# Attention followed by a gated product on one core: the products take the batches in pairs, one half of d_ff at a time

## The chip, the cores and the metric

The kernel runs on one core of a Trainium2 chip. The time is the device time of the whole kernel in microseconds (us). TensorE is called PE below (and PEld where it loads weights), VectorE DVE, ScalarE ACT, GpSimd POOL, and SyncE, which issues all DMAs here, SP.

## The reference

Causal attention over 4 batches, 12 heads, 448 positions, head dimension 64, all float32:

```
scores = where(mask, -1e9, (q @ k.T) / 8)
attn   = exp(scores - max) ; attn = attn / (sum + 1e-9)
x      = (attn @ v), the heads side by side: 1792 tokens x 768
out    = ((x @ w_a) * (x @ w_b)) @ w_out        # 768 -> 1536 -> 768
```

The weights arrive as 64-bit words, which the kernel turns into float32 on the chip with integer and float operations.

## The kernel before

**Units.** The weights come in 36 units of 128 x 768: 12 of w_a and 12 of w_b, alternating (units 0 to 23), and 12 of w_out (24 to 35). `load_words` fetches the 64-bit words of a unit, `convert_unit` makes float32 of it (five DVE operations and one of ACT, lines 303 to 315) and keeps a copy in DRAM (`w_keep`). `load_kept` fetches that copy again when the unit is used a second time. `split_unit` splits a unit into a high part (`w_hi`, ACT, line 255) and a rest (`w_lo`, DVE, line 271); attention's output x and the gated product g are split in the same way. A product of one 128-row slice k is then three matmuls of 448 columns, high x high, high x rest, rest x high (`products`, line 498), and a unit for one batch is 18 of these.

**Attention of two heads.** A step works on a pair of heads of a batch; there are 24 pairs of heads. `scores` multiplies q and k in four blocks of rows (line 375), takes the negative maximum on DVE (388) and the exponential with its sum on ACT (394), forms the reciprocal of the sum on DVE (408, 411) and normalises on POOL (419). `turn` transposes the causal part of each head in 10 PE operations (440): 7 work on 128 rows of the array, 3 on 64 rows, the lower half of a block on the diagonal. ACT copies the result out of PSUM in two pieces per head (255, `pt<-t`). `values` multiplies with v (461), and ACT and DVE split the result into `x_hi` and `x_lo`. Three buffers `p` hold the heads between the maximum and the transposition.

**Order.** `order` (line 476) lists which unit is used for which batch: units 0 to 13 for batch 0 alone, 14 to 23 for batches 0 and 1 in turn, 0 to 13 for batch 1, units 24 to 35 for batches 0 and 1, then all 36 for batch 2 and all 36 for batch 3. Attention of batch 0 stands in front of the products; that of batches 1, 2 and 3 is dealt out among them by `attend`, one pair of heads every 11, 26 and 34 slices k (`AT`). Three units are converted in front (`PACE`). Every operation is entered with an estimated duration, and `Plan.order` (line 123) puts the operations of each engine in an order by a list schedule: among the operations that are ready by its estimates it takes the one entered first. Each engine, and SP's DMA queue, then works through its list in order. PSUM has three banks `m` for products (batch 0's scores use them too), two for scores, two for transposes and one for values.

Of the kernel before, what the change touches and what calls it, by code (L numbers as in the profile page):

```python
# [18 lines left out]
P = 128  # L19
# [6 lines left out]
UW = KT * P  # L26

# [6 lines left out]
SOLO = 14  # L34

APART = (3, 0, 0, 0)


AT = ((2, 11), (262, 26), (436, 34))
STEP = (8, 3, 8)  # L40

LATE = (27, 2)

PACE = (0, 1, 1, 1, 0, 0, 0)
LEAD = (3, 2)
# [3 lines left out]
HOLD = (10e3, 5e3)  # L49
# [166 lines left out]
def causal_attention_then_gated_product(  # L216
# [24 lines left out]
    ident = const.tile([P, P], F32, name="ident")  # L241
    mask = const.tile([P, S], F32, name="mask")
# [3 lines left out]
    g_hi = const.tile([P, FT, S], F32R, name="g_hi")  # L246
    g_lo = const.tile([P, FT, S], F32R, name="g_lo")
    w_keep = [dram.tile([P, UW], F32, name=f"w_keep{u}") for u in range(NU)]

    g_keep = [dram.tile([P, S], F32, name=f"g_keep{f}") for f in range(FT)]  # L250
# [26 lines left out]
    w_64, w_32, w_parts = {}, {}, {}  # L277

    def load_words(u):
        t = sb("w_64", 3, [P, UW, 2], U32)  # L280
        load(P * UW * 8, lambda: t.t.rearrange("p n t -> p (n t)"), lambda: w[u].bitcast(U32), [], [t])
        w_64[u] = t

    def load_kept(n):
        t = sb("w_32", 3, [P, UW])
        u = fetched[n]
        load(P * UW * 4, lambda: t.t, lambda: w_keep[u], [("keep", u)], [t])
        w_32[n] = t

    def convert_unit(u, n=None):  # L290
        t = w_64.pop(u)
# [11 lines left out]
        plan.op("dve", dve_ns(UW, 2), lambda: nc.vector.tensor_scalar(  # L303
            out=e.t, in0=high(), scalar1=0x7FF00000, scalar2=None, op0=ALU.bitwise_and), [t], [e])
        plan.op("dve", dve_ns(UW, 2), lambda: nc.vector.tensor_scalar(
            out=m.t, in0=high(), scalar1=0x000FFFFF, scalar2=0x00100000,
            op0=ALU.bitwise_and, op1=ALU.bitwise_or), [t], [m])
        plan.op("act", act_ns(UW), lambda: nc.scalar.activation(
            e.t, e.t, AF.Copy, bias=-896.0 * 2**23, scale=8.0), [e], [e])
        plan.op("dve", dve_ns(UW), lambda: nc.vector.scalar_tensor_tensor(  # L310
            out=r(), in0=m.t, scalar=2.0**32, in1=low(), op0=ALU.mult, op1=ALU.add), [m, t], [m])
        plan.op("dve", dve_ns(UW), lambda: nc.vector.scalar_tensor_tensor(  # L312
            out=e.t, in0=high(), scalar=0x80000000, in1=e.t,
            op0=ALU.bitwise_and, op1=ALU.bitwise_or), [t, e], [e])
        plan.op("dve", dve_ns(UW), lambda: nc.vector.scalar_tensor_tensor(  # L315
# [3 lines left out]
        if n is not None:  # L319
            w_32[n] = wt  # L320

    def split_unit(n):
        if n >= len(fetched):
            return
        t = w_32.pop(n)
# [8 lines left out]
        w_parts[n] = hi, lo  # L334
# [17 lines left out]
    def scores(b, hp):  # L352
# [14 lines left out]
        for pair, w0 in (((3, 0), 448), ((2, 1), 320)):  # L367
            banks = [bank("m", 3) if b == 0 and w0 == 320 else bank(f"s{j}") for j in range(2)]
# [44 lines left out]
        for ci in pairs.values():  # L413
            for j in range(2):
                for i in ci:
                    def norm(i=i, j=j, p=p_of[b, hp, j]):
                        s = rc.t[:D if i == 0 else P, j, i:i + 1]
                        pc = chunk(p, i)
                        return nc.gpsimd.tensor_scalar(  # L419
# [3 lines left out]
                    plan.op("pool", pool_ns(QE[i]), norm, [(rc, j, i)], [(p_of[b, hp, j], i)])  # L423


    spots = (((0, 0), (3, 448)), ((1, 0), (2, 320)))

    def turn(b, hp, j):
        p = p_of.pop((b, hp, j))
        for n, spot in enumerate(spots):  # L430
            t = bank(f"t{n}")
            for c, o in spot:
                for i in range(c, 4):

                    q0 = max(QS[i], 128 * c)
                    r = slice(q0 - QS[i], P)
                    at = o + q0 - 128 * c

                    def mm(c=c, i=i, r=r, at=at, t=t):
# [6 lines left out]
                    plan.op("pe", (P - r.start) / 1.2, mm, [(p, i), "ident"], [t])  # L446
            full = sb("pt", 6, [P, 512])
            copy("act", 512, lambda full=full: full.t, lambda t=t: t.t, [t], [full], True)
            pt[j, n] = full

    def values(b, hp, x):
        ps, vt = bank("pv"), v_of.pop((b, hp))
        x_hi, x_lo = x
        parts = dict(pt)
        for c in range(4):
# [3 lines left out]
            def mm(c=c, n=n, o=o):  # L459
                for j in range(2):  # L460
# [8 lines left out]
        copy("act", S, lambda: x_hi.t[:, hp, :], lambda: ps.t[:, :S], [ps], [(x_hi, hp)], True)  # L469
        two_input("dve", S, lambda: x_lo.t[:, hp, :], lambda: ps.t[:, :S],  # L470
                  lambda: x_hi.t[:, hp, :].bitcast(F32), ALU.subtract, [ps, (x_hi, hp)], [(x_lo, hp)])
# [4 lines left out]
    order = (  # L476
        [(0, u) for u in range(SOLO)]
        + [(b, u) for u in range(SOLO, NA) for b in range(2)]
        + [(1, u) for u in range(SOLO)]
        + [(b, u) for b in range(2) for u in range(NA, NU)]  # L480
        + [(b, u) for b in range(2, B) for u in range(NU)]
    )

    fetched = [u for n, (b, u) in enumerate(order) if n == 0 or order[n - 1][1] != u]
    xs, a_sb, g_wait = {}, {}, []
# [4 lines left out]
    def part_g(f, g, key):  # L490
        copy("act", S, lambda: g_hi[:, f, :], g, [key], [("g_hi", f)])
        two_input("dve", S, lambda: g_lo[:, f, :], g,
                  lambda: g_hi[:, f, :].bitcast(F32), ALU.subtract, [key, ("g_hi", f)], [("g_lo", f)])

    def products(ps, parts, k, hi, lo, first, last, keys):
# [7 lines left out]
        plan.op("pe", 3 * pe_ns(S), mm, [parts[0], parts[1], *keys], [ps])  # L503

    fetches, m = {}, -1
    for n, (_, u) in enumerate(order):
        if m < 0 or fetched[m] != u:
            m += 1
            fetches[n] = m

    def turned(n):

        ahead = fetches.get(n, NA) + LEAD[0]
        late, r = divmod(n - LATE[0], LATE[1])
        return [ahead] * (ahead < NA) + [NA + late] * (r == 0 and 0 <= late < NU - NA)

    in_turn = list(range(LEAD[0])) + [u for n in range(len(order)) for u in turned(n)]
    to_load, to_turn = iter(in_turn), iter(in_turn)

# [4 lines left out]

    def convert_next():
        u = next(to_turn)
        plan.soonest = HOLD[0] + HOLD[1] * u if u < NA else 0.0
        convert_unit(u, u if u < NA else None)
        plan.soonest = 0.0
        load_next()  # L530

    def uses():

        m = -1
        for n, (b, u) in enumerate(order):
            new = n in fetches
            m = fetches.get(n, m)
            for _ in turned(n):
                convert_next()
            if new and NA <= m + LEAD[0] < len(fetched):  # L540
                load_kept(m + LEAD[0])
            if n == 2 * NA - SOLO:

                for tag in ("x_hi", "x_lo"):
                    g_wait.append(sb(tag, 2, [P, KT, S]))
            back = SOLO // 2 + n - (2 * NA - SOLO)
            if SOLO // 2 <= back < FT:
                g, fk = g_wait[back // KT], back % KT
                load(P * S * 4, lambda g=g, fk=fk: g.t[:, fk, :], lambda f=back: g_keep[f], [("g", back)], [(g, fk)])
            parts = w_parts[m]  # L550
            x_hi, x_lo = xs[b]
            f, half = divmod(u, 2)
            if f < FT or half == 0:
                ps = bank("m", 3)
            for k in range(KT):
                if f < FT:
                    products(ps, parts, k, lambda k=k, x=x_hi: x.t[:, k, :], lambda k=k, x=x_lo: x.t[:, k, :],
                             k == 0, k == KT - 1, [(x_hi, k), (x_lo, k)])
                else:
                    ft = half * KT + k  # L560
                    products(ps, parts, k, lambda ft=ft: g_hi[:, ft, :], lambda ft=ft: g_lo[:, ft, :],
                             ft == 0, ft == FT - 1, [("g_hi", ft), ("g_lo", ft)])
                    if b == 0 and u >= NU - 2:
                        g, fk = g_wait[ft // KT], ft % KT
                        part_g(ft, lambda g=g, fk=fk: g.t[:, fk, :], (g, fk))
                if k == 1 and new:
                    split_unit(m + LEAD[1])
                if k == KT - 1:
                    if f >= FT:
                        if half == 1:  # L570
                            o_sb = sb("mid", 4, [P, S])
                            copy("act", S, lambda o=o_sb: o.t, lambda ps=ps: ps.t[:, :S], [ps], [o_sb], True)
                            load(P * S * 4, lambda b=b, f=f: out[b, f - FT], lambda o=o_sb: o.t, [o_sb], [])
                    elif half == 0:
                        a_sb[b] = sb("mid", 4, [P, S])
                        copy("act", S, lambda a=a_sb[b]: a.t, lambda ps=ps: ps.t[:, :S], [ps], [a_sb[b]], True)
                    else:
                        if b == 1 and f < SOLO // 2:
                            wait, fk = g_wait[f // KT], f % KT
                            g, key = (lambda w=wait, fk=fk: w.t[:, fk, :]), (wait, fk)  # L580
                        else:
                            key = sb("mid", 4, [P, S])
# [108 lines left out]
```

## Time and profile before

| | |
|---|---|
| median of 3 runs | 732.8 us (732.65, 732.8, 743.98) |
| the profiled execution's own time | 733.78 us |
| its span, first to last instruction | 732.0 us |
| PE busy | 719.5 us of it |
| DVE busy | 430.5 us |
| ACT busy | 360.3 us |
| POOL busy | 138.9 us |
| granted PE clock, mean | 0.995 |

Busy time of PE is the union of its instructions from start to modelled end; matmuls overlap each other, so a busy PE can still be doing less than its best pace. The other engines' busy times can be taken as work done. The "mean ns" of an instruction runs from its start to its end, and two neighbours on one engine may overlap by some 80 to 100 ns.

### The profile page before, as it was taken

Reading aid. Unit: us, or ns where it says so; the run is one execution under the profiler, and the core shown is the slowest. Engines: PE = TensorE matmul, PEld = TensorE weight load, DVE = VectorE, ACT = ScalarE, POOL = GpSimd, SP = SyncE. Lnnn points to the kernel's source line nnn. Section 1 sums busy time; section 2 is a strip of 40 time slices with the busy share of each in tenths; the row PEclk is TensorE's granted clock in tenths of the full one; section 3 lists DMA queues with packets and bytes.
Section 4 is the critical chain, followed back from the end, with each engine's and each line's share of the span. In section 5 each row is a group of like instructions: output and inputs, shape, how many; then the busy total and the mean of one; then the engine's idle time right before and its main releaser. Section 6 shows DMA issues by size and latency. Waiting matters only on the chain.

```text
span 732.0 us, 10834 instructions
## 1 busy us (share of the span) xinstructions
PE 719.5 (98%) x3884; PEld 598.3 (82%) x3884; DVE 430.5 (59%) x911; ACT 360.3 (49%) x795; POOL 138.9 (19%) x201
## 2 busy tenths in 40 slices
PE   8999999899999999999999999999999999999998
PEld 6567667668999998778887888878878889999997
DVE  7888989799987798333843244543543424343321
ACT  6987565664333345544755353554554443333321
POOL 5661544440000002112420102201302200000000
PEclk9999999899999999999999999999999999999999
DMA  8637455456687875334343332323214223333341
GB/s 315 223 127 230 142 198 177 167 168 219 233 276 262 279 250 201 112 112 138 108 159 122 128 118 93 115 67 108 90 56 144 91 99 108 107 109 108 120 133 39
DMA packets 43446, 110.75 MB, mean 151 GB/s; under 512 B 4992, under 2 KB 20096, under 8 KB 43392
## 3 DMA queue, kind: packets, MB, share of 16 engines
q1 hardware_dynamic: 43392, 110.05, 45.1%
q8 instruction: 31, 0.51, 0.3%
q14 instruction: 23, 0.19, 0.1%
HBM read 89.23 MB, written 20.81 MB: 150 GB/s over the span
## 4 chain that ended last, share of the span: by engine, by line
PE 90%; POOL 5%; DVE 3%; ACT 1%; issue 1%; POOLq 0%; DVEq 0%
PE m L498 68%; PE t L440 9%; PE s L375 6%; PE pv L461 5%; POOL p L419 5%; DVE p L388 1%; ACT p L394 1%; DVE w_m L310 1%; PE fill L634 1%; PE m L375 0%; DVE w_e L312 0%; DVE w L315 0%; DVE w_lo L271 0%; DVE x_lo L271 0%; DVE g_lo L271 0%
## 5 line engine op out<-in xcount | busy, mean ns | idle before, releaser
L271 DVE TENSOR_TENSOR w_lo<-w,w_hi 128x768 fp32r<-128x768 f32 x134 | 141.8, 1059 | 173.5 <-ACT w_hi L255 171.1
L419 POOL TENSOR_SCALAR p<-p,rc 128x448 f32<-128x448 f32 (+1 forms) x192 | 136.3, 728 | 442.2 <-DVE rc L411 316.3
L498 PE MATMUL m<-x_hi,w_hi 128*128 128x448 f32 x576 | 216.2, 375 | 0.0
L498 PE MATMUL m<-x_hi,w_lo 128*128 128x448 f32 x576 | 211.1, 367 | 0.0
L498 PE MATMUL m<-x_lo,w_hi 128*128 128x448 f32 x576 | 211.0, 366 | 0.0
L255 ACT ACTIVATE w_hi<-w 128x768 fp32r<-128x768 f32 x134 | 112.6, 840 | 105.2 <-issue 52.7
L498 PEld LDWEIGHTS m<-x_hi,w_hi 128*128 128x128 f32 x576 | 110.0, 191 | 10.8 <-issue 1.3
L394 ACT ACTIVATE p<-p,nm 128x448 f32<-128x448 f32 (+2 forms) x192 | 95.2, 498 | 44.4 <-DVE nm L388 44.1
L498 PEld LDWEIGHTS m<-x_hi,w_lo 128*128 128x128 f32 x576 | 108.6, 189 | 8.9
L498 PEld LDWEIGHTS m<-x_lo,w_hi 128*128 128x128 f32 x576 | 108.8, 189 | 7.9
L498 PE MATMUL m<-g_hi,w_hi 128*128 128x448 f32 x288 | 107.4, 373 | 0.0
L498 PE MATMUL m<-g_lo,w_hi 128*128 128x448 f32 x288 | 104.5, 363 | 0.0
L498 PE MATMUL m<-g_hi,w_lo 128*128 128x448 f32 x288 | 104.1, 361 | 0.0
L255 ACT ACTIVATE mid<-m 128x448 f32<-128x448 f32 x72 | 39.1, 543 | 125.4 <-PE m L498 125.2
L440 PE MATMUL t<-ident,p 128*128 128x128 f32 (+1 forms) x480 | 87.0, 285 | 8.1 <-POOL p L419 8.0
L440 PEld LDWEIGHTS t<-ident,p 128*128 128x128 f32 (+1 forms) x480 | 56.2, 141 | 41.4 <-issue 17.0
L388 DVE CUSTOM_DVE_ANT_0 p<-s,mask 128x448 f32<-128x448 f32 (+3 forms) x168 | 61.5, 416 | 48.4 <-PE s L375 42.7
L255 ACT ACTIVATE pt<-t 128x512 f32<-128x512 f32 x96 | 56.4, 597 | 63.8 <-PE t L440 63.4
L498 PEld LDWEIGHTS m<-g_hi,w_hi 128*128 128x128 f32 x288 | 55.1, 191 | 5.8 <-issue 1.6
L498 PEld LDWEIGHTS m<-g_hi,w_lo 128*128 128x128 f32 x288 | 53.9, 187 | 3.7
L498 PEld LDWEIGHTS m<-g_lo,w_hi 128*128 128x128 f32 x288 | 54.2, 188 | 2.8
L375 PE MATMUL s<-raw 64*128 64x448 f32 (+3 forms) x336 | 50.3, 413 | 0.0
(45 smaller groups left out, 506.3 us busy)
## 6 DMA issues: line engine op xcount, KB each, us to landing
w<-w_keep SPq DMA_DIRECT2D x110, 384.0 KB, 2.9
w<-w SPq DMA_DIRECT2D x36, 768.0 KB, 5.2
w_keep<-w SPq DMA_DIRECT2D x36, 384.0 KB, 3.8
raw<-qT SPq DMA_DIRECT2D x24, 224.0 KB, 2.5
raw<-kT SPq DMA_DIRECT2D x24, 224.0 KB, 2.7
out<-mid SPq DMA_DIRECT2D x24, 224.0 KB, 2.0
v<-v SPq DMA_DIRECT2D x24, 192.0 KB, 2.8
g_keep<-mid SPq DMA_DIRECT2D x5, 224.0 KB, 4.6
```

The source lines that it names most:

```text
L255: return nc.scalar.activation(o(), i(), AF.Copy)
L271: plan.op(engine, ns, lambda: e.tensor_tensor(out=o(), in0=a(), in1=b(), op=op), reads, writes)
L310: plan.op("dve", dve_ns(UW), lambda: nc.vector.scalar_tensor_tensor(out=r(), in0=m.t, scalar=2.0**32, in1=low(), op0=ALU.mult, op1=ALU.add ...
L375: r = nc.tensor.matmul(banks[j].t[:, at[i]], q[:, QS[i]:QS[i] + P], k[:, 0:QE[i]], start=True, stop=True)
L388: return nc.vector.tensor_tensor_reduce(out=chunk(p, i), in0=bk.t[:r, at[i]], in1=m, scale=-0.125, scalar=3.0e38, op0=ALU.add, op1=ALU.min ...
L394: return nc.scalar.activation(chunk(p, i), chunk(p, i), AF.Exp, bias=nm.t[:r, j, i:i + 1], scale=-1.0, accum_out=sm.t[:r, j, i:i + 1],)
L419: return nc.gpsimd.tensor_scalar(out=pc, in0=pc, scalar1=s, scalar2=1.0, op0=ALU.mult, op1=ALU.mult)
L440: return nc.tensor.matmul(t.t[:, at:at + P - r.start], p.t[r, PO[i] + 128 * c:PO[i] + 128 * (c + 1)], ident[r, r], is_transpose=True, star ...
L461: r = nc.tensor.matmul(ps.t[j * D:(j + 1) * D, 128 * c:S], vt.t[:, c, j, :], parts[j, n].t[:, o:o + S - 128 * c], start=c == 0, stop=c == 3,)
L498: r = nc.tensor.matmul(ps.t[:, :S], a.t[:, k, :], x(), start=first and n == 0, stop=last and n == 2)
L634: plan.filler = lambda: nc.tensor.matmul(fill[:, 0:P], warm, warm, start=True, stop=True)
```

## The change

- `order` becomes: for batches 0 and 1 together, w_a and w_b of the first half of d_ff (12 units), w_out's first half (6 units), the second halves in the same way, and then the same 36 units for batches 2 and 3. Each unit is used for both batches of the pair, so it is fetched and split twice in the kernel instead of up to four times. g is kept for two batches and half of d_ff.
- The first half's result of w_out goes to DRAM (`o_keep`) and comes back to be added on DVE when the second half is done.
- Attention of batches 0 and 1 stands in front of all products; that of batches 2 and 3 is dealt out in the first pass, one pair of heads every 34 slices (`AT`). Its x goes to DRAM (`x_keep`), and comes back and is split near the end of that pass (`take_x`).
- Transposes all work on 128 rows. Those on the diagonal use `swapped`, an identity with its halves exchanged, so that the part that is not wanted falls where the next transpose writes over it; the order within a bank changes for that.
- For batches 0 and 1 one of the two copies out of PSUM per head goes from ACT to DVE (`TAKE`). For batches 2 and 3 ACT normalises in place of POOL (`NORM`). The reciprocals of batch 1 are formed in four pieces, as those of batch 0 were (`APART`).
- Two units are converted in front, after its ninth and eleventh step, not before 40 and 60 us (`PACE`, `HOLD`); the planner's estimates for conversions (660, 840, 1030 ns), products (203 ns) and transposes (109 ns) are new.

```diff
-APART = (3, 0, 0, 0)
-AT = ((2, 11), (262, 26), (436, 34))
+APART = (3, 3, 0, 0)
+NORM = ("pool", "pool", "act", "act")
+TAKE = (("act", "dve"), ("act", "dve"), ("act", "act"), ("act", "act"))
+AT = (2, 34)
...
-PACE = (0, 1, 1, 1, 0, 0, 0)
-LEAD = (3, 2)
+PACE = (0, 0, 0, 0, 0, 0, 0, 0, 1, 0, 1, 0, 0)
+LEAD = (2, 1)
-HOLD = (10e3, 5e3)
+HOLD = (40e3, 20e3)
...
-    g_hi = const.tile([P, FT, S], F32R, name="g_hi")
+    g_hi = const.tile([P, 2, HF, S], F32R, name="g_hi")
...
-            banks = [bank("m", 3) if b == 0 and w0 == 320 else bank(f"s{j}") for j in range(2)]
+            banks = [bank("m", 3) if b < 2 and w0 == 320 else bank(f"s{j}") for j in range(2)]
...
+                        if NORM[b] == "act":
+                            return nc.scalar.activation(pc, pc, AF.Copy, scale=s)
...
-    spots = (((0, 0), (3, 448)), ((1, 0), (2, 320)))
+    spots = (((3, 448), (0, 0)), ((2, 320), (1, 0)))
...
-                    q0 = max(QS[i], 128 * c)
-                    r = slice(q0 - QS[i], P)
-                    at = o + q0 - 128 * c
+                    swap = c == i and c in (1, 2)
+                    at = o + QS[i] - 128 * c + (D if swap else 0)
...
-                            t.t[:, at:at + P - r.start],
-                            p.t[r, PO[i] + 128 * c:PO[i] + 128 * (c + 1)],
-                            ident[r, r], is_transpose=True, start=True, stop=True,
+                            t.t[:, at:at + P],
+                            p.t[:, PO[i] + 128 * c:PO[i] + 128 * (c + 1)],
+                            swapped if swap else ident, is_transpose=True, start=True, stop=True,
...
-            copy("act", 512, lambda full=full: full.t, lambda t=t: t.t, [t], [full], True)
+            copy(TAKE[b][n], 512, lambda full=full: full.t, lambda t=t: t.t, [t], [full], True)
...
+        if x is None:
+            t = sb("mid", 5, [P, S])
+            copy("act", S, lambda: t.t, lambda: ps.t[:, :S], [ps], [t], True)
+            load(P * S * 4, lambda: x_keep[b - 2][hp], lambda: t.t, [t], [("xk", b, hp)])
...
+    def take_x(b, x, k):
+        t = sb("acc", 3, [P, S])
+        load(P * S * 4, lambda: t.t, lambda: x_keep[b - 2][k], [("xk", b, k)], [t])
+        split_x(x, k, lambda: t.t, t, False)
...
+    order = []
+    for _ in range(2):
+        for h in range(2):
+            order += [("ab"[r], f) for f in range(h * HF, (h + 1) * HF) for r in range(2)]
+            order += [("o", 2 * e + h) for e in range(ET)]
...
+                if kind == "o" and h == 1:
+                    acc = sb("acc", 3, [P, S])
+                    load(P * S * 4, lambda t=acc: t.t, lambda b=b, e=e: o_keep[b][e], [("o", b, e)], [acc])
...
+                            two_input("dve", S, lambda t=t: t.t, lambda ps=ps: ps.t[:, :S],
+                                      lambda a=acc: a.t, ALU.add, [ps, acc], [t])
+                        if kind == "o":
+                            load(P * S * 4, (lambda b=b, e=e: out[b, e]) if h else (lambda b=b, e=e: o_keep[b][e]),
+                                 lambda t=t: t.t, [t], [] if h else [("o", b, e)])
...
+    pairs = [(b, hp) for b in range(2) for hp in range(NP)]
...
+    for i in range(len(pairs) + 1):
...
+        if i >= 1:
+            turn(*pairs[i - 1], 0)
+            turn(*pairs[i - 1], 1)
+        if i < len(pairs):
+            scores(*pairs[i])
+        if i >= 1:
+            values(*pairs[i - 1], xs[pairs[i - 1][0]])
+        for _ in range(PACE[i]):
+            convert_next()
```

## Rows read from the trace of the kernel before

**Rows 1.** The page's busy times by engine, and its chain of work that ended last, by engine and by line.

```profile
PE 719.5 (98%) x3884; PEld 598.3 (82%) x3884; DVE 430.5 (59%) x911; ACT 360.3 (49%) x795; POOL 138.9 (19%) x201
...
PE 90%; POOL 5%; DVE 3%; ACT 1%; issue 1%; POOLq 0%; DVEq 0%
```

**Rows 2.** Busy time of each engine in stretches of the span: PE, PEld, DVE, ACT, POOL with the instructions in brackets, then the granted PE clock, the DMA engines' share and GB/s.

```profile
17.97:63.16 45.19, 44.36 (x293) 27.32 (x292) 40.75 (x140) 37.91 (x110) 25.24 (x38) 1.00 0.56 185
...
0.00:167.54 167.54, 158.36 (x933) 109.80 (x933) 144.87 (x387) 113.59 (x299) 78.27 (x105) 0.98 0.57 195
167.54:279.00 111.46, 111.46 (x552) 103.05 (x551) 97.06 (x135) 43.60 (x62) 0.00 (x0) 1.00 0.73 250
...
140.00:160.00 20.00, 17.00 (x82) 12.34 (x83) 13.98 (x32) 10.19 (x26) 9.59 (x12) 0.83 0.42 132
...
180.00:260.00 80.00, 80.00 (x397) 74.15 (x395) 67.93 (x94) 28.86 (x42) 0.00 (x0) 1.00 0.77 265
```

**Rows 3.** The same view for the products' matmuls alone (line 498): the stretch, PE's busy time in them and their count, clock, DMA.

```profile
60.00:160.00 100.00, 55.45 (x231) 0.97 0.52 175
0.00:167.54 167.54, 63.94 (x265) 0.98 0.57 195
167.54:279.00 111.46, 111.46 (x549) 1.00 0.73 250
...
598.31:732.00 133.69, 130.35 (x645) 1.00 0.32 102
```

**Rows 4.** The same view for the matmuls with v (line 461), 16 of which are one pair of heads.

```profile
60.00:160.00 100.00, 12.14 (x96) 0.97 0.52 175
...
0.00:167.54 167.54, 23.84 (x192) 0.98 0.57 195
```

**Rows 5.** The chain that ended last in order of time (start us, us, what): the start, and the starts of batch 0's multiplications with v (17.97, 26.01, 35.62, 43.11), with the two turns between the last two; the pieces left out there are scores on PE.

```profile
5.36 1.17 PE s L375 x8
...
17.97 1.88 PE pv L461 x16
...
26.01 1.88 PE pv L461 x16
...
35.62 1.88 PE pv L461 x16
37.50 1.68 PE t L440 x10
...
40.47 1.69 PE t L440 x10
...
43.11 1.88 PE pv L461 x16
```

**Rows 6.** The same chain where attention of batch 3 lies among products (one turn and the products behind it), and its last long piece.

```profile
449.68 1.53 PE t L440 x10
451.21 1.85 PE m L498 x9
...
598.31 130.36 PE m L498 x645
```

**Rows 7.** PE's instructions in order of time within one `turn` and just behind it (start us, us, operation, rows*columns of the array, shape, count), from narrow windows; the one line with bars is the second of the two on 64 rows alone, in the view by line (busy us, mean ns | idle before).

```profile
449.51 0.27 PE L440 MATMUL t<-ident,p 128*128 128x128 f32 x1
...
449.51 0.60 PE L440 MATMUL t<-ident,p 128*128 128x128 f32 x4
...
450.04 0.33 PE L440 MATMUL t<-ident,p 64*128 64x64 f32 x2
...
L440 PE MATMUL t<-ident,p 64*128 64x64 f32 x1 | 0.2, 222 | 0.0
...
450.96 0.45 PE L498 MATMUL m<-x_hi,w_hi 128*128 128x448 f32 x1
451.25 0.36 PE L498 MATMUL m<-x_lo,w_hi 128*128 128x448 f32 x1
```

**Rows 8.** Groups of instructions by line: busy us, mean ns of one | idle time of the engine just before, and who ended it.

```profile
L394 ACT ACTIVATE p<-p,nm 128x448 f32<-128x448 f32 (+2 forms) x192 | 95.2, 498 | 44.4 <-DVE nm L388 44.1
L255 ACT ACTIVATE pt<-t 128x512 f32<-128x512 f32 x96 | 56.4, 597 | 63.8 <-PE t L440 63.4
L255 ACT ACTIVATE w_hi<-w 128x768 fp32r<-128x768 f32 x134 | 112.6, 840 | 105.2 <-issue 52.7 <-PE m L498 31.5 <-DMA w<-w_keep 12.1
L255 ACT ACTIVATE g_hi<-mid 128x448 fp32r<-128x448 f32 x36 | 20.7, 576 | 14.7 <-DVE mid L271 14.6
L271 DVE TENSOR_TENSOR w_lo<-w,w_hi 128x768 fp32r<-128x768 f32 x134 | 141.8, 1059 | 173.5 <-ACT w_hi L255 171.1
L310 DVE SCALAR_TENSOR_TENSOR w_m<-w_m,w 128x768 f32<-128x768 uint32 x36 | 37.0, 1028 | 0.2
L303 DVE TENSOR_SCALAR w_e<-w 128x768 uint32<-128x768 uint32 x36 | 20.9, 580 | 0.1
L271 DVE TENSOR_TENSOR mid<-m,mid 128x448 f32<-128x448 f32 x41 | 25.5, 622 | 31.9 <-PE m L498 31.9
L388 DVE CUSTOM_DVE_ANT_0 p<-s,mask 128x448 f32<-128x448 f32 (+3 forms) x168 | 61.5, 416 | 48.4 <-PE s L375 42.7 <-PE t L440 5.1
...
L408 DVE TENSOR_SCALAR rc<-sm 128x2 f32<-128x2 f32 x24 | 5.4, 230 | 2.2 <-ACT p L394 2.0
L411 DVE RECIPROCAL rc<-rc 128x2 f32<-128x2 f32 x24 | 3.6, 155 | 0.1
L419 POOL TENSOR_SCALAR p<-p,rc 64x64 f32<-64x64 f32 x48 | 30.0, 624 | 0.0
```

**Rows 9.** The chain again, at the place where the granted clock fell, and behind it.

```profile
137.95 4.19 POOL p L419 x2
...
142.66 1.12 PE m L498 x3
143.78 2.36 PE t L440 x9
...
159.89 1.65 PE t L440 x9
```

**Rows 10.** DMA issues: size of one, median us from issue to landing.

```profile
g_keep<-mid SPq DMA_DIRECT2D x5, 224.0 KB, 4.6
x_lo<-g_keep SPq DMA_DIRECT2D x5, 224.0 KB, 3.2
```

More of the change, by code (lines that the diff above doesn't have):

```diff
@@ L26 @@
 UW = KT * P
+HF = FT // 2
 QS = (0, 64, 192, 320)
@@ L241, in causal_attention_then_gated_product @@
     ident = const.tile([P, P], F32, name="ident")
+    swapped = const.tile([P, P], F32, name="swapped")
     mask = const.tile([P, S], F32, name="mask")
@@ L468, in values @@
                     [(vt, 1 if c == 3 else 0), parts[0, n], parts[1, n]], [ps])
[L469 to L482, printed above, removed]
@@ L484, in causal_attention_then_gated_product, with split_x @@
-    fetched = [u for n, (b, u) in enumerate(order) if n == 0 or order[n - 1][1] != u]
-    xs, a_sb, g_wait = {}, {}, []
+        if x is None:
+            t = sb("mid", 5, [P, S])
+            copy("act", S, lambda: t.t, lambda: ps.t[:, :S], [ps], [t], True)
+            load(P * S * 4, lambda: x_keep[b - 2][hp], lambda: t.t, [t], [("xk", b, hp)])
+        else:
+            split_x(x, hp, lambda: ps.t[:, :S], ps, True)
+    def split_x(x, k, i, key, in_psum):
+        x_hi, x_lo = x
+        copy("act", S, lambda: x_hi.t[:, k, :], i, [key], [(x_hi, k)], in_psum)
+        two_input("dve", S, lambda: x_lo.t[:, k, :], i, lambda: x_hi.t[:, k, :].bitcast(F32), ALU.subtract,
+                  [key, (x_hi, k)], [(x_lo, k)])
@@ new lines, in take_x @@
+    def take_x(b, x, k):
[7 more added lines that the diff above has]
+            order += [("o", 2 * e + h) for e in range(ET)]
+    place = {"a": lambda n: 2 * n, "b": lambda n: 2 * n + 1, "o": lambda n: NA + n}
+    in_turn = [place[kind](n) for kind, n in order]
@@ L501, in mm @@
             return r
[L503 to L518, printed above, removed]
+        plan.op("pe", 3 * 203, mm, [parts[0], parts[1], *keys], [ps])
+    to_load = iter(in_turn[:NU])
     def load_next():
@@ L523, in load_next @@
             load_words(u)
+    turned, parted = [0], [0]
     def convert_next():
[L526 to L530, printed above, removed]
-    def uses():
[L534 to L553, printed above, removed]
-                ps = bank("m", 3)
[L555 to L576, printed above, removed]
-                    else:
-                        if b == 1 and f < SOLO // 2:
-                            wait, fk = g_wait[f // KT], f % KT
-                            g, key = (lambda w=wait, fk=fk: w.t[:, fk, :]), (wait, fk)
-                        else:
-                            key = sb("mid", 4, [P, S])
-                            g = lambda t=key: t.t
-                        two_input("dve", S, g, lambda ps=ps: ps.t[:, :S],
-                                  lambda a=a_sb[b]: a.t, ALU.mult, [ps, a_sb[b]], [key])
-                        if b != 1:
-                            part_g(f, g, key)
-                        elif f >= SOLO // 2:
-                            load(P * S * 4, lambda f=f: g_keep[f], g, [key], [("g", f)])
-                yield
@@ L592, in attend @@
-    def attend(g):
-        for b in range(1, B):
-            at, each = AT[b - 1]
-            hp, r = divmod(g - at, each)
-            if not 0 <= hp <= NP:
-                continue
-            if hp == 0 and r == 0:
-                load_pair(b, 0)
-            if hp < NP and r == STEP[0]:
-                scores(b, hp)
-                if hp + 1 < NP:
-                    load_pair(b, hp + 1)
-            if hp > 0 and r == STEP[1]:
-                turn(b, hp - 1, 0)
-                turn(b, hp - 1, 1)
-            if hp > 0 and r == STEP[2]:
-                if hp == 1:
-                    xs[b] = x_parts()
-                values(b, hp - 1, xs[b])
+        n = turned[0]
@@ new lines, in attend, with at @@
+    def attend(g):
+        n, r = divmod(g - AT[0], AT[1])
+        if not 0 <= n <= 2 * NP:
+            return
+        def at(n):
+            return 2 + n // NP, n % NP
+        if n == 0 and r == 0:
+            load_pair(*at(0))
+        if n < 2 * NP and r == STEP[0]:
+            scores(*at(n))
+            if n + 1 < 2 * NP:
+                load_pair(*at(n + 1))
+        if n > 0 and r == STEP[1]:
+            turn(*at(n - 1), 0)
+            turn(*at(n - 1), 1)
+        if n > 0 and r == STEP[2]:
+            values(*at(n - 1), None)
@@ L622, in causal_attention_then_gated_product, with start_identity @@
     plan.op("pool", 800, start_mask, [], ["mask"])
-    plan.op("pool", 600, lambda: make_identity(nc, ident), [], ["ident"])
+    def start_identity():
+        make_identity(nc, ident)
+        for a, b in ((0, D), (D, 0)):
+            nc.gpsimd.tensor_scalar(
+                out=swapped[:, a:a + D], in0=ident[:, b:b + D], scalar1=1.0, scalar2=1.0, op0=ALU.mult, op1=ALU.mult
+            )
+    plan.op("pool", 1200, start_identity, [], ["ident"])
     nc.gpsimd.memset(p_buf[0], 0.0)
@@ L634, in causal_attention_then_gated_product @@
     plan.filler = lambda: nc.tensor.matmul(fill[:, 0:P], warm, warm, start=True, stop=True)
-    xs[0] = x_parts()
+    pairs = [(b, hp) for b in range(2) for hp in range(NP)]
+    for b in range(2):
+        xs[b] = x_parts()
     for c in START:
@@ L639, in causal_attention_then_gated_product @@
         else:
-            load_pair(0, int(c))
-    for i in range(NP + 1):
-        if i + 1 < NP and (0, i + 1) not in v_of:
-            load_pair(0, i + 1)
+            load_pair(*pairs[int(c)])
+    for i in range(len(pairs) + 1):
+        if i + 1 < len(pairs) and pairs[i + 1] not in v_of:
+            load_pair(*pairs[i + 1])
         if i >= 1:
-            turn(0, i - 1, 0)
-            turn(0, i - 1, 1)
-        if i < NP:
-            scores(0, i)
+            turn(*pairs[i - 1], 0)
+            turn(*pairs[i - 1], 1)
+        if i < len(pairs):
+            scores(*pairs[i])
         if i >= 1:
-            values(0, i - 1, xs[0])
+            values(*pairs[i - 1], xs[pairs[i - 1][0]])
         for _ in range(PACE[i]):
             convert_next()
-    split_unit(0)
-    split_unit(1)
+    for _ in range(LEAD[1]):
+        split_next()
     for g, _ in enumerate(uses()):
```

103 lines of the change are left out of this document (71 added, 32 removed).

## The prediction

> **What bounds the kernel now.** PE is busy 98% of the span and holds 90% of the chain that ended last; POOL's 5% is the largest other piece [rows 1]. Busy time doesn't say how much PE could still save, so I count its work at its best pace. In the two stretches with products alone 549 matmuls follow each other in 111.46 us, 203 ns each, and at the end 645 in 130.36 us, 202 ns each [rows 3, 6]. The kernel has 4 batches x 36 units x 18 = 2592 of them: at 202.5 ns 524.9 us. A pair of heads in front takes PE from 35.62 to 43.11 us, 7.49 us without a gap (all pieces of the chain there are PE's) [rows 5]; 24 pairs at 7.5 us are 180 us. The last matmul ends at 598.31 + 130.36 = 728.67, which leaves 3.3 us of 732.0 for the copy out and the last DMA. 524.9 + 180 + 3.3 = 708.2, so PE loses only 732.0 - 708.2 = 23.8 us in the whole kernel. They lie in the first 167.54 us, where 265 matmuls (53.8 us) and 192 / 16 = 12 pairs of heads (90 us) fill 143.8 us [rows 3, 4]; that leaves 23.7 us. About 14 of them come before the first multiplication with v at 17.97: the first scores start at 5.36, and the first pair of heads has nothing beside it [rows 5]. Another part lies between 60 and 160 us: 231 matmuls (46.9 us) and 6 pairs (45 us) leave 8.1 us [rows 3, 4]. From 17.97 to 63.16 PE is busy 44.36 of 45.19 us [rows 2].
>
> So there are two things that can be gained: the 24 us of loss, of which the start stays, and a cheaper pace of PE's own work.
>
> **Products, order and weights.** The count of matmuls stays 2592, and a unit is still 18 for a batch: nothing on PE. Splits of units fall from 134 to 72, by 62 x 1.06 us of DVE and 62 x 0.84 us of ACT [rows 8]. These engines aren't what PE waits for after 167 us, so I cost that at zero. The pattern of the new first pass has been run: from 180 to 260 us units are converted and used for two batches in turn, DVE is busy 67.93 of 80 us, and PE does 397 matmuls without a gap [rows 2].
>
> **Transposes.** A `turn` has 7 transposes on 128 rows and 3 on 64. The first four, on 128 rows, take 0.60 us together where one takes 0.27, so they start (0.60 - 0.27) / 3 = 0.11 us apart; two on 64 rows, half as wide, take 0.33 us together, of which the second has 0.22, so it starts 0.11 us behind the first [rows 7]. The fourth starts at 449.84, and the first of 64 rows at 450.04, 0.20 later. Behind the last one the first two products start 0.29 us apart (450.96 to 451.25), against the 0.20 of products among themselves [rows 3, 7]. So a change of the number of rows costs PE a gap each time. In the chain a turn takes 1.53 us [rows 6]; ten at 0.11 us are 1.1. With all ten on 128 rows I take 0.43 us off each of 48 turns: **20.6 us** (at least 0, as a rival below has it). A pair of heads falls from 7.5 to 6.64 us. The Trainium skill speaks against this step: by TensorEngine Tiling (Array Packing), section Performance Considerations, a contraction of 64 can be tiled by rows, with up to twice the speed, and the change gives that up. The trace shows no such speed for these transposes, and by the rule the sum would be some 28 us higher (see the rivals). The product that follows and the copies out of PSUM are as before. `swapped` costs POOL two small operations before 5 us, under the load of q and k; zero, and 2 x 0.62 = 1.2 us by POOL's normalisation of 64 columns if that cover is gone [rows 8].
>
> **The front.** Its 12 pairs of heads now run with no products beside them. I take the first values at 17.97 as before, and a period from there. It can't be below PE's 6.64 us, and the periods of before are 8.04, 9.61 and 7.49 [rows 5], in all of which three conversions, slow transposes and DVE-delayed POOL have a part. What other engines need for a pair: ACT 95.2 / 24 = 3.97 for the exponentials, two copies of 0.60, 0.58 for x by g's split, 5.7 us in all (6.9 before). DVE: 8 x 61.5 / 168 = 2.9 us for the maxima, at most 4 x (0.23 + 0.16) = 1.5 for the reciprocals, 0.62 for x, and two copies of 512 columns out of PSUM, which no row shows; the nearest is the product of 448 columns out of PSUM at 0.62 us, and I take 0.7 each (below by 0.1, above by 0.3, as an SBUF operation of 768 columns takes 1.03) [rows 8]. That is 6.4 us, with overlap of neighbours nearer 5.3. A conversion is 3 x 1.02 + 2 x 0.58 = 4.2 us of DVE, and two or three of them come after 40 us. So DVE is close behind PE, and ACT has room. I take 6.8 us, nearest to PE's floor, since PE had no gap to speak of even with the conversions [rows 2]. The front ends at 17.97 + 11 x 6.8 + 1.88 = 94.7 us; PE's work in it is 12 x 6.64 = 79.7, and 15.0 us are lost, against 23.7 before: **8.7 us** gained. Products of batch 0 can only fill the last two periods, as their banks `m` are taken by the scores of batch 1.
>
> **The first pass.** Over 34 slices PE does 102 matmuls (20.7 us) and a pair of heads (6.6): 27.3 us. DVE has 2.83 units x (4.2 + 1.06) = 14.9, 2.83 x 1.25 for g, and 3.4 for the heads' maxima and reciprocals: 21.8, 80%. ACT has 2.83 x 1.68 + 2.83 x 1.12 + 3.97 + 5 x 0.60, and eight normalisations. Those no row shows on ACT: at most the exponentials' 3.97, at least 3.3 by the copy of 448 columns at 0.576 scaled to the four widths [rows 8]; I take 3.6, in all 18.5 of 27.3. That is beside PE's work, with 17 us between a pair's scores and its turn. If ACT were late, the turn's ten transposes would wait, and the products entered behind it with them. x and half results go through DRAM: 36 stores more and 36 loads, by the g that does so now 4.6 and 3.2 us each way [rows 10]. The last x is stored some 25 slices (15 us) before it is needed; on SP's queue each store also holds up what lies behind it until its data are there, weights two units (14 us) ahead. I take 2 us for passes' edges; at least 0, at most 16 (below).
>
> **Sum.** 524.9 + 24 x 6.64 + 15.0 + 3.3 + 2 = 704.6 us of span, 27.4 less than 732.0. The execution took 1.8 us more than its span, and the median is 1.0 below that execution: 704.6 + 1.8 - 1.0, in round numbers 705 us.
>
> **Rivals.**
> - *The front runs at the slow pace.* If the buffers `p`, each held from the maximum to the transposition, and POOL set 8.04 to 9.61 us a pair, as in two of three periods seen, 11 x (1.24 to 2.8) give 719 to 736. For it: DVE 40.75 and ACT 37.91 of 45.19 us in front [rows 2]. Against it: conversions did that, and they are gone until 40 us.
> - *The first pass loses at each pair of heads*, as between 60 and 160 us: 8.1 / 6 = 1.35 us, x 12 = 16: 719 with the 2 us already in. For it: conversions and attention meet again. Against: there a unit lasted half as long on PE, and POOL had the norms in DVE's way.
> - *The 128-row transposes save nothing*, that is, the gaps come from loading `p` and not from the change of rows: 705 + 21 = 726. If 64-row transposes also ran at double pace, 144 x 0.055 = 8 us come on top: 734. That is what the rule of the Trainium skill named above (TensorEngine Tiling) would give.
> - *The clock falls in front* (slower than before). The granted clock is 1.00 up to 60 us and fell in one place, 0.83 over 140 to 160, after PE had waited for two POOL operations of 4.19 us [rows 2, 9]. At the lower level (1.2 GHz) three products took 1.12 us against 0.61, nine transposes 2.36 against 1.65 [rows 6, 9]. A pair of heads would need 2.2 x 1.43 + 4.44 x 1.84 = 11.3 us, 4.5 more than I take; x 12 = 54: 759. It decides for slower than 747.5 from ten of the twelve pairs on. Against it: batch 0's front, 3.4 of 7.5 us transposes, held 1.00 [rows 2, 5]. By the Trainium skill, TensorE: Matmul & The Clock Gate, section Part 4: PE-mode transpose, transposes do not count as PE activity in the same way, which makes a front of attention alone the place to fear; 54 us is what that would cost.
>
> **Numbers.** Forecast 66%, slow front 11%, first pass 10%, no gain on transposes 6%, clock 5%, and 2% for several at once. 2% either way, about what a measurement of this kernel can tell from no change, are 718.1 and 747.5. Faster is the forecast, the lower ends of the slow front and the first pass (8 points together), 0.74; slower is the clock and a slow front with a lossy pass, 0.06; same is the rest, 0.20. The range reaches down to a front at PE's floor, no loss at edges and products at 200 ns in part (together -8: 697), with 2 us more for an earlier first value: 695; up through the first pass and half of the slow front: 726.
>
> **What would show it.** Turns of 1.1 us in the chain; the 24 pairs' PE work 159 us and not 180; starts of `pv` 6.6 to 7.0 us apart in front; the first product near 90 us; from there to the end products and heads without a gap; clock 1.00 up to the end. Wrong if the starts of `pv` are 8 us apart, if PE waits in the first pass for `pt`, `w_hi` or `x`, or if transposes of 128 rows come 0.16 us apart throughout.

## The result, and the profile after

The changed kernel takes **710.91 us** (median of 4 runs, 710.7 to 711.34), against 734.3 for the kernel before on the same chip: ratio 0.968, interval 0.964 to 0.9715. Forecast were 705 us, 695 to 726, and faster by over 2%. The span is 708.9 us where 704.6 were expected. Executions of one kernel differ by how long its granted clock is low: those of the kernel before span 729.5 to 742.4 us, at mean clocks of 1.00 to 0.986, and all four of the change are at 1.00.

From the page after: span and busy times, the granted clock by fortieths, and the chain by engine.

```profile
span 708.9 us, 10638 instructions
...
PE 698.3 (99%) x3884; PEld 599.5 (85%) x3884; DVE 390.7 (55%) x933; ACT 341.8 (48%) x817; POOL 56.0 (8%) x107
...
PEclk9999999999999999999999999999999999999999
...
PE 91%; ACT 3%; DVE 3%; POOL 2%; issue 1%; POOLq 0%; ACTq 0%
```

Beside [rows 1], PE's busy time fell by 21.2 us with the same 3884 instructions, and the clock stayed up throughout.

The stretches of the new kernel, beside [rows 2]: the front in two parts, the first pass, in the columns of that view; then the products alone (line 511) up to the front's end.

```profile
17.78:60.28 42.50, 41.35 (x318) 26.89 (x316) 37.89 (x154) 31.45 (x107) 21.97 (x45) 1.00 0.33 102
60.28:105.95 45.67, 42.15 (x290) 28.06 (x290) 41.67 (x147) 32.23 (x99) 25.68 (x40) 1.00 0.46 147
105.95:432.24 326.29, 326.29 (x1849) 281.98 (x1845) 227.19 (x479) 206.42 (x484) 0.00 (x0) 1.00 0.51 174
...
0.00:105.95 105.95, 8.67 (x33) 1.00 0.48 157
```

In the first pass PE has no gap, with DVE 70% and ACT 63% busy. In front it has some, and DVE is busy 89 to 91%. The chain in order of time: first and last values of the front, one pair of heads among products, beside [rows 6], and the last pass.

```profile
17.85 1.88 PE pv L461 x16
...
104.14 1.88 PE pv L461 x16
...
186.47 1.88 PE pv L461 x16
...
190.21 17.22 PE m L511 x84
207.43 1.09 PE t L441 x10
208.52 0.61 PE m L511 x3
209.13 1.09 PE t L441 x10
210.22 2.42 PE m L511 x12
212.64 1.12 PE s L373 x8
213.76 1.88 PE pv L461 x16
...
432.24 272.98 PE m L511 x1335
```

A turn takes 1.09 us, where it took 1.53; the starts of the values in the first pass lie 27.3 us apart (186.47 to 213.76), which is 102 products and 6.64 us for the heads. The front's are (104.14 - 17.85) / 11 = 7.84 us apart, with 33 products in between (6.7 us): 7.24 without them, where I had taken 6.8. The prediction's sign of being wrong, starts 8 us apart, was nearly met.

### The profile page after: what moved, and what is told of

It is laid out like the page before. It is cut to its first block, busy times and chain, and to the rows that moved or that the text cites. A ratio compares the mean times of both kernels' runs of the same rounds, so it can differ in the third digit from the quotient of the medians.

```text
span 708.9 us, 10638 instructions
## 1 busy us (share of the span) xinstructions
PE 698.3 (99%) x3884; PEld 599.5 (85%) x3884; DVE 390.7 (55%) x933; ACT 341.8 (48%) x817; POOL 56.0 (8%) x107
## 4 chain that ended last, share of the span: by engine, by line
PE 91%; ACT 3%; DVE 3%; POOL 2%; issue 1%; POOLq 0%; ACTq 0%
PE m L511 75%; PE t L441 6%; PE s L373 5%; PE pv L461 4%; ACT p L392 2%; POOL p L419 2%; DVE p L386 1%; PE fill L637 1%; ACT pt L257 1%; PE m L373 1%; DVE rc L406 1%; DVE pt L265 1%; DVE w_m L306 0%; DVE rc L409 0%; POOLq L691 0%
## 5 line engine op out<-in xcount | busy, mean ns | idle before, releaser
L273 DVE TENSOR_TENSOR w_lo<-w,w_hi 128x768 fp32r<-128x768 f32 x72 | 69.0, 958 | 145.2 <-ACT w_hi L257 137.2
L511 PEld LDWEIGHTS m<-x_hi,w_hi 128*128 128x128 f32 x576 | 108.2, 188 | 12.6 <-issue 2.7
L392 ACT ACTIVATE p<-p,nm 128x448 f32<-128x448 f32 (+1 forms) x192 | 95.2, 498 | 43.8 <-DVE nm L386 43.8
L257 ACT ACTIVATE w_hi<-w 128x768 fp32r<-128x768 f32 x72 | 60.5, 840 | 56.9 <-PE m L511 56.6
L441 PE MATMUL t<-ident,p 128*128 128x128 f32 x384 | 64.3, 277 | 4.3 <-ACT pt L257 2.9
L386 DVE CUSTOM_DVE_ANT_0 p<-s,mask 128x448 f32<-128x448 f32 (+3 forms) x144 | 53.0, 415 | 26.9 <-PE s L373 26.8
L441 PEld LDWEIGHTS t<-ident,p 128*128 128x128 f32 x384 | 46.4, 140 | 14.0 <-POOL p L419 5.5
L273 DVE TENSOR_TENSOR mid<-m,mid 128x448 f32<-128x448 f32 x48 | 29.9, 623 | 50.2 <-PE m L511 50.2
L419 POOL TENSOR_SCALAR p<-p,rc 128x320 f32<-128x320 f32 (+2 forms) x96 | 53.0, 569 | 43.5 <-ACT p L392 26.7
L257 ACT ACTIVATE pt<-t 128x512 f32<-128x512 f32 x72 | 41.2, 593 | 31.2 <-PE t L441 30.8
```

What stands on the lines that cost most here:

```text
L257: return nc.scalar.activation(o(), i(), AF.Copy)
L273: plan.op(engine, ns, lambda: e.tensor_tensor(out=o(), in0=a(), in1=b(), op=op), reads, writes)
L386: return nc.vector.tensor_tensor_reduce(out=chunk(p, i), in0=bk.t[:r, at[i]], in1=m, scale=-0.125, scalar=3.0e38, op0=ALU.add, op1=ALU.min ...
L392: return nc.scalar.activation(chunk(p, i), chunk(p, i), AF.Exp, bias=nm.t[:r, j, i:i + 1], scale=-1.0, accum_out=sm.t[:r, j, i:i + 1],)
L419: return nc.gpsimd.tensor_scalar(out=pc, in0=pc, scalar1=s, scalar2=1.0, op0=ALU.mult, op1=ALU.mult)
L441: return nc.tensor.matmul(t.t[:, at:at + P], p.t[:, PO[i] + 128 * c:PO[i] + 128 * (c + 1)], swapped if swap else ident, is_transpose=True, ...
```

## The experiments

Two questions stood open: how much of the 23 us the transposes bring and how much the new order, and what the front waits for. Medians in us, ratios to the kernel before on the same chip.

**Transposes undone (e1)**: in the change, `turn` and `spots` as before.

```diff
-    spots = (((3, 448), (0, 0)), ((2, 320), (1, 0)))
+    spots = (((0, 0), (3, 448)), ((1, 0), (2, 320)))
...
+                    q0 = max(QS[i], 128 * c)
+                    r = slice(q0 - QS[i], P)
...
```

> The changed kernel with its transposes put back to 64 rows on the diagonal (order in the banks as before), all else as changed. If a change of the number of rows costs PE 0.43 us a turn, and PE is the bound nearly everywhere, 48 turns give the 20.6 us back: 711 + 20 = about 731 us, and a turn in the middle of the products takes 1.5 us again in the chain. If the order by pairs brought the gain and the transposes little, it stays below 715.

731.44, ratio 0.994 (0.991 to 0.997), the same as before by a bar of 2%; span 729.5. So 729.5 - 708.9 = 20.6 us came back, the forecast term; that it agrees to the decimal is chance. In this execution the granted clock fell in the front, to the lower level (0.50, 1.2 GHz):

```profile
57.50:62.50 5.00, 5.00 (x16) 1.97 (x16) 4.17 (x21) 3.76 (x13) 1.61 (x4) 0.50 0.00 0
```

The three of nine executions at clock 1.00 span 726.8 to 727.5, some 18 us above the change. From the last values of the front to those of the first pass e1 takes 11.6 us more, near the 24 x 0.44 = 10.6 of its turns; in the front, where PE waits for other engines as well, some 6 us come back at clock 1.00, not 10. All the rest of the change, with 64-row transposes, is worth 0.6%.

**Transposes alone (e2)**: the same lines put into the kernel before.

> The kernel before with the 128-row transposes alone (the swapped identity, the other order in the banks), all else as before. By the theory of the transposes 734 - 20 = 712 to 716 us, so that all the rest of the change is worth 0 to 5 us. If the order by pairs is needed for the gain (PE waits for POOL at each pair of heads between 60 and 160 us, and a faster turn only waits longer), 720 to 730 us.

724.96, ratio 0.984 (0.979 to 0.988), clear of no change and undecided at 2%; span 723.2. Less than half of the 20.6 us by span, half by the medians. The products-only stretch, which began at 167.54 [rows 2], begins at 165.96: of some 10 us in the first 12 pairs 1.6 were gained, with 259 products done by then and not 265. The stretch from 60 to 160 us before; then of that run, and 140 to 160:

```profile
60.00:160.00 100.00, 93.53 (x518) 67.39 (x517) 87.31 (x193) 62.91 (x159) 41.32 (x45) 0.97 0.52 175
```

```profile
60.00:160.00 100.00, 89.45 (x521) 66.74 (x520) 89.19 (x192) 61.97 (x159) 46.89 (x48) 0.97 0.54 184
140.00:160.00 20.00, 14.68 (x82) 11.64 (x81) 15.45 (x33) 8.92 (x22) 12.06 (x11) 0.83 0.44 154
```

and its chain there:

```profile
105.02 7.50 POOL p L420 x8
...
120.22 5.04 POOL p L420 x4
...
149.47 6.50 POOL p L420
```

PE is busy 89 us of 100, where it was 94: the faster turns wait longer for POOL's normalisation. One such operation took 6.50 us at 149.47. DVE's conversions run without a pause there until 155.45, and the operation ends 0.5 us later: that they kept POOL from its data was the theory for the next two runs.

**Old order, batch 1 normalised by ACT, with 128-row transposes (e12) and without (e13)**:

```diff
+                        if b == 1:
+                            return nc.scalar.activation(pc, pc, AF.Copy, scale=s)
...
```

> e2_before_full_rows (the order of before with 128-row transposes) with batch 1's normalisation on ACT. In e2 the first 12 pairs of heads ended at 165.9 us, 1.6 us earlier than in the kernel before, though their transposes take 10 us less, and PE waits for POOL there. If POOL, held up by DVE's conversions, is what took those 10 us, this gives 8 to 10 us on e2: about 715. If DVE itself (89% busy there, conversions among the maxima) is behind, 0 to 3 us: 722 to 725.

> The kernel before with batch 1's normalisation on ACT alone: 64-row transposes, the old order. PE waits for POOL 8 us in the first 167 us and loses about 24 in all, about 14 of them before 18 us. If the moved normalisation removes the waits between 60 and 160 us and no more, 8 to 10 us less than before: about 725. If it gives the 15 us that it gave on top of the 128-row transposes, about 719; if the two only work together, 731 or more.

e12: 710.2, ratio 0.967 (0.961 to 0.974), span 707.6. e13: 723.22, ratio 0.985 (0.978 to 0.992), undecided at 2%, span 721.1. The stretch 60 to 160 us, e12 first:

```profile
60.00:160.00 100.00, 99.68 (x602) 78.25 (x599) 91.04 (x210) 88.20 (x219) 0.00 (x0) 1.00 0.63 211
```

```profile
60.00:160.00 100.00, 99.96 (x585) 74.17 (x584) 86.81 (x207) 87.85 (x219) 0.00 (x0) 1.00 0.60 195
```

PE is busy throughout, though DVE does as much as before. So DVE itself was not late; POOL was, and by more than expected: 15.6 us of span between e2 and e12. Some 4 of them come and go with the clock: it fell behind PE's longest wait in e2 (the 0.83 above), and e2's one execution at 0.999 spans 719.1. That it is the conversions which hold POOL up is argued from the operation at 149.47; no run leaves them out. **The old order with these two edits is as fast as the whole change.** By spans: before 732.0, transposes alone -8.8, ACT alone -10.9, both -24.4, the whole change -23.1. That the two need each other for the 4.7 us between is not shown: these executions of before and e2 were at a clock of 0.995, the others at 1.00, and by medians against before the three are -10.5, -12.3 and -23.8, a plain sum but for 1.1 us. That the pairs' order brings anything on top of the two edits is not shown by any run. It stands in for the ACT edit: with 128-row transposes and POOL normalising throughout it takes 712.38 (e4 below) against e2's 724.96. With 64-row transposes it does so worse (spans at clock 1.00: e1 726.8 to 727.5, e13 720.6 and 721.1).

**The three 64-row transposes side by side (e3)**, on e1:

```diff
...
+            cells = cells + halves if n == 0 else halves + cells
...
```

> As e1_half_rows, with the three 64-row transposes of a turn next to each other: the last of the first bank, the first two of the second. A turn then changes the number of rows twice and not four times. If each change costs about 0.11 us, half of the 0.43 us comes back: 10 us less than e1_half_rows, about 721. If a 64-row transpose is slow in itself (its load of p, or its place in the array), nothing changes against e1_half_rows.

712.48, ratio 0.969 (0.966 to 0.973). More came back than expected. Turns and last pieces in its chain, then in e1's:

```profile
210.08 1.24 PE t L445 x10
...
437.66 269.55 PE m L515 x1335
```

```profile
219.91 1.53 PE t L441 x10
...
452.79 272.98 PE m L511 x1335
```

With one change to 64 rows and back a turn takes 1.24, with two 1.53, with none 1.09 for ten of 0.109. So a change there and back costs 0.29 us, and a 64-row transpose among its like (1.24 - 0.29 - 7 x 0.109) / 3 = 0.062 us, near half of one on 128 rows, which is also twice as wide. The rival "slow in itself" is out. 48 x 0.29 = 13.9 us; another 3.4 are the pace of the last pass, 202 ns a product and not 204.5 (next run); and e1's clock had fallen.

**A matmul of another shape before the last pass's products (e7)**:

```diff
+                if first == 2 and b == 2 and kind == "a" and f in (0, HF):
+                    plan.op("pe", 200, lambda ps=ps: nc.tensor.matmul(
+                        ps.t[:, 0:D], ident[0:D, :], ident[0:D, 0:D], start=True, stop=True), ["ident"], [ps])
```

> The changed kernel with two small matmuls on 64 rows added, one each where the last pass goes over from w_out's products to w_a's. In the last pass the matmuls on x follow each other every 206.7 ns, in the first pass and in the kernel before mostly every 202.7. If that pace is set by how PE goes over to these products (directly from those on g, or after a matmul of another shape), the 432 x 2 matmuls return to 202.7 ns: 864 x 4.0 ns = 3.5 us less, less 2 x 0.4 us for the two, about 708 us. If it depends on what the other engines or DMAs do in that pass, the pace stays at 206.7 ns and the time at 711 us or 1 us above.

709.32, ratio 0.964 (0.961 to 0.967). Products in two stretches of the last pass, the change first:

```profile
445.00:525.00 80.00, 80.00 (x388) 1.00 0.16 51
580.00:655.00 75.00, 75.00 (x364) 1.00 0.17 53
```

```profile
445.00:525.00 80.00, 80.00 (x396) 1.00 0.19 55
580.00:655.00 75.00, 75.00 (x372) 1.00 0.17 53
```

8 more in 80 us and in 75: an edit in front of the run of products settles its pace, for 432 matmuls, while the other engines do the same work. But what stands right before it isn't all. e3 goes from the products on g straight to those on x, as the change does, and has the faster pace. And the products on x that follow the matmuls with v took 203 ns in the kernel before (549 in 111.46 us [rows 3]), and 207 in e2:

```profile
165.96 114.89 PE m L499 x555
```

Of the 3.5 us about 1.6 show in the median, since the front was 1.75 us later in the profiled execution (the values at 104.14 start at 105.89 there). Up to 83.60 the two executions agree; then the granted clock is 0.56 until 87.5 us, where it is 1.00 in the change. The chain there, the change first:

```profile
83.60 1.31 PE t L441 x10
84.91 0.95 PE s L373 x4
```

```profile
83.60 2.31 PE t L441 x10
85.92 1.58 PE s L373 x4
```

The two of four executions at clock 1.00 span 706.4 and 706.5, 2.4 to 3.2 us below the change's four (708.9 to 709.6): about the 2.7 forecast.

**POOL normalises batches 2 and 3 (e4)**: `NORM = ("pool",) * 4`.

> The changed kernel with the normalisation of batches 2 and 3 put back from ACT to POOL. By the theory that PE alone bounds the first pass (no gap there, ACT 63% and DVE 70% busy) nothing changes: 710 to 713 us. If POOL's operations hold up DVE's conversions, as between 60 and 160 us before, the first pass gets gaps at each pair of heads: up to 12 x 1.35 = 16 us more.

712.38, ratio 0.965 (0.961 to 0.969). PE is busy all of the first pass here as well (326.29 of 326.29 us): in this order ACT's normalisation isn't needed. The profiled execution has a fall of the clock in front, as e7's.

**The front: copies on ACT (e5), no addition (e6), four buffers p (e9)**:

```diff
-TAKE = (("act", "dve"), ("act", "dve"), ("act", "act"), ("act", "act"))
+TAKE = (("act", "act"), ("act", "act"), ("act", "act"), ("act", "act"))
```

```diff
-                plan.op("dve", 69 + n, lambda sj=sj, si=si: nc.vector.tensor_scalar_add(
-                    rc.t[:, sj, si], sm.t[:, sj, si], 1.0e-9),
+                plan.op("dve", 115 + n, lambda sj=sj, si=si: nc.vector.reciprocal(
+                    rc.t[:, sj, si], sm.t[:, sj, si]),
...
```

```diff
-    NPB, NVB = 3, 3
+    NPB, NVB = 4, 3
...
-        t = sb("raw", 4, [P, 2, S])
+        t = sb("raw", 3, [P, 2, S])
```

> The changed kernel with both copies of a head out of PSUM on ACT in front as well. If DVE is what sets the pace of the front (its busy share is 0.89 and ACT's 0.74 from 17.8 to 60.3 us), 12 x 1.4 us of DVE less make it shorter by 3 to 6 us. If ACT sets it, ACT rises from 5.2 to 6.4 us a pair and the time by 0 to 5 us.

> The changed kernel with the reciprocal taken of the sum itself: the addition of 1e-9 to the sums is left out everywhere. In front these additions take DVE 272 ns each on average though they touch 2 numbers a row (the reciprocals 156 ns), 11 us in all. If the front is bound by DVE and the latency through the reciprocal, 4 to 8 us less; if it is bound by the buffers p or by POOL, 0 to 2 us less.

> The changed kernel with four buffers p in place of three (and three buffers for q and k in place of four, to make room). If the front's pace is set by the three buffers, each held from the maximum to the transposition, the pairs come at PE's 6.64 us plus the products and the front gets 4 to 6 us shorter: about 706. If it is set by DVE or POOL, within 1 us of 711.

708.84 (0.960, 0.956 to 0.964), 708.33 (0.960, 0.955 to 0.965), 710.14 (0.962, 0.958 to 0.966). Against the change's 710.9, measured on another chip, that is 2 to 3 us each for DVE's work, less than expected if DVE sets the pace, and less than 1 for the buffer, as expected if the buffers do not. But in all four executions of e9 the mean clock was 0.997, which by an estimate (0.3% of 708 us) costs 2 us: alone, the fourth buffer may be worth up to 3. The front's first stretch in e5:

```profile
17.78:60.28 42.50, 42.20 (x320) 27.14 (x320) 32.23 (x156) 38.92 (x125) 22.64 (x44) 1.00 0.37 114
```

DVE falls from 37.89 to 32.23 us and PE's gaps from 1.2 to 0.3; ACT is now at 92%.

**Together: e5 + e6 + e7 (e10), and with four buffers (e11)**.

> e5, e6 and e7 together on the changed kernel: copies out of PSUM on ACT, no addition of 1e-9 (the largest score of a row gives exp(0) = 1, so a sum is at least 1 and 1e-9 is lost in float32), the odd matmuls before the last pass's products on x. If the two DVE savings take from the same waits, the front is bound by PE after the first of them and the sum is 711 - 2.6 - 2.4 = 706; if they add up, 711 - 2.1 - 2.6 - 2.4 = 704.

> e10 with four buffers p and three for q and k. If PE bounds the front in e10, no change (within 1 us of it); if the three buffers are what is left of its waits, 1 to 3 us less than e10.

e10: 708.16, ratio 0.961 (0.957 to 0.965), a miss: no better than e5 or e6 alone. Its front ends at 100.03 us, where e5's ends at 98.57, which uses up what e7's edit gains in the last pass. e11: **702.35, ratio 0.953 (0.949 to 0.957)**, faster than both kernels by more than their intervals, and a miss the other way: 5.8 us where 1 to 3 were the most expected. With DVE's work lessened, and ACT's grown by the copies, three buffers still hold the front up. A pair of heads of e11's front in the chain:

```profile
38.59 1.88 PE pv L459 x16
40.47 1.24 PE t L439 x10
41.71 1.12 PE s L373 x8
42.83 1.24 PE t L439 x10
44.07 1.06 PE m L373 x8
45.13 1.88 PE pv L459 x16
```

45.13 - 38.59 = 6.54 us, all of it PE's: the floor that the prediction put at 6.64. (A turn among heads takes 1.24 us; it took 1.68 before [rows 5].)

## Why the prediction was right, and where its steps were not

- **What bounds the kernel**: right. PE's work at its best pace and 24 us of loss explain before and after.
- **Transposes, 20.6 us**: right in size on PE: 1.09 us a turn, 48 x 0.44 = 21.1. Of the span they give some 18, and 20.6 in an execution of e1 with a fall of the clock. The reading behind it was half wrong. "The trace shows no such speed for these transposes" was read from two 64-row transposes 0.11 apart, of which the first still carried the change; in a row they follow at 0.062 (e3). And the 0.29 us between the first two products isn't part of the change of rows; it is there after as well (208.28 and 208.56 in the new kernel's order of time). The Trainium skill, TensorEngine Tiling (Array Packing), section Key Properties, says that changing the tiling mode drains the engine: by e3 that is 0.29 us there and back here. Three 64-row transposes save 0.14 us, and their changes cost 0.58. Whether the same page's gain for small contractions has a part in the 0.14 is not shown, as these transposes are also half as wide.
- **The front**: the step that failed in size. "I take 6.8 us, nearest to PE's floor": 7.24 without the products, so 106.02 - 12 x 6.64 - 6.7 = 19.6 us were lost, not 15.0. DVE, which I had "close behind PE", was at 89%: a copy took 0.68 us, as assumed, and an addition on two numbers a row 0.27. The premise, that PE had no gap to speak of, didn't carry it: here PE is busy 41.35 of 42.50 us as well, and each pair takes 0.6 us more than the floor. What sets the pace is DVE, ACT and the three buffers together: no single edit reaches the floor; e11 does, at least from 32 to 58 us. The groups of those copies and additions in the front:

```profile
L265 DVE COPY pt<-t 128x512 f32<-128x512 f32 x23 | 15.7, 681 | 3.7 <-PE t L441 3.5
...
L406 DVE TENSOR_SCALAR rc<-sm 128x2 f32<-128x2 f32 x42 | 11.0, 272 | 2.6 <-ACT p L392 2.4
```

- **"8.7 us gained" by the order**: the loss was moved rightly, its owner was not. I set 60 to 160 us down as something the new order removes. e12 and e13 show that it was POOL's normalisation, and that moving it to ACT removes it in the old order too. With 19.6 lost in front, the gain there was 4.1 us.
- **First pass, 2 us at the edges**: none were lost; e4 shows that ACT's part in it was not needed.
- **Products at 202.5 ns**: 1335 in 272.98 us are 204.5 in the last pass, 2.7 us more, as those on x ran at 206.7 (e7); in the first pass 201.4, with 6.64 us taken off for each pair of heads, 1.3 less.
- **Sum**: 704.6 + 4.6 (front) - 2 (edges) + 2.7 - 1.3 (pace) + 0.4 (tail: 708.9 - 705.22 = 3.7) = 709.0, measured 708.9. That 704.6 came so near is in part luck: the front's 4.6 us stood against the edges' 2 and the pace.
- **Rivals**: the slow front came about by a third (7.24 lies between the 6.8 taken and 8.04); the others didn't, in the change itself.

## What to carry to other kernels

Count the bound engine's work at its best pace before reading its busy share: here 98% busy hid 21 us of PE's time in 144 small matmuls. Keep matmuls of one height together, or make them all full height; what a change costs is read from a run with half as many. Savings needn't add: e5, e6 and e7 took 2.1, 2.6 and 1.6 us alone and 2.8 together, and a fourth buffer 0.8 alone and 5.8 on top of them. So test each alone and all together, and test the old order with the small edits before crediting a new order. Compare executions at the same granted clock before reading a difference of 2 or 3 us.

## What was not expected of the hardware

- A run of equal matmuls keeps one of two paces, 202.7 or 206.7 ns for 448 columns on x, and holds it for hundreds. One small matmul on 64 rows in front makes it the faster (e7); but e3 has the faster without it, and e2 the slower behind the matmuls with v, where before has the faster. What sets it is open.
- One POOL operation on 448 columns took 6.50 us beside DVE's conversions, where the mean of all of its kind before was 0.81, and a DVE addition on two numbers 0.27 us beside POOL. The Trainium skill, SBUF — State Buffer, section Who interferes with whom, says that the two share a pair of ports, which one instruction can hold to its end. Here the wait went on through eight operations of DVE in a row. e12 and e13, with POOL idle there, agree as far as they go: PE's 10 us of gaps in 100 are gone.
- In the change the granted clock held 1.00 through 106 us of attention, transposes and all; but the same front lost it in e1 (0.50 from 57.5 to 62.5 us), e4 and e7 (0.57 to 0.75 over 82.5 to 87.5) and e9 (0.50 from 97.5 to 100), each time behind a wait of PE for POOL of 1.0 to 1.9 us, as in the kernel before and e2 behind 2.7 and 4.8. A wait alone doesn't decide: the change has the one of e7, 1.0 us up to 81.90, and kept its clock. In e1 it was back at 1.00 by 65 us, with nothing but attention on PE. The Trainium skill, TensorE: Matmul & The Clock Gate, section Part 4: PE-mode transpose, would have had one fear a fall from the transposes; these falls stand behind waits, and in e11's front, attention almost alone and hardly a wait, it held 1.00.
